# Early token planes, loads at step heads and staggered conversions in a fused attention, gated and normalised layer

## The chip, the cores and the metric

One core of one Trainium2 chip runs the kernel. The metric is device time in microseconds of one execution. TensorE (PE) does the matmuls, VectorE (DVE), ScalarE (ACT) and GpSimd (POOL) the work on elements, and SyncE (SP) issues most DMAs; each engine runs its instructions in order.

## What is computed

```
scores = q @ k.T / 8 + bias(positions)            # 4 batches, 8 heads, 576 tokens, 64 features
x  = softmax(scores) @ v, heads side by side      # 2304 tokens x 512
x2 = ((x @ w1) * (x @ w2)) @ w3 @ w_out           # 512 -> 1024 -> 1024 -> 512
h  = x2 @ w_in;  s = h * softmax(h)               # 1024
out = layernorm(s) * g @ w_out2                   # 2304 x 512
```

All in float32. Weights reach the chip as 64-bit words, and are converted to float32 on it. Products run in float32r as three matmuls, high x high, high x low and low x high: each operand is split into a rounded part (a ScalarE copy) and the rest (a subtraction).

## The kernel before

**Bias** builds the position biases in DRAM. **Attention** runs 16 pairs (two heads of one batch) as one pipeline of slots, ten to a pair: `slot(s)` does scores for one block of keys, the exponent of an earlier one, transposes (`tp`, evicted by L477 on ScalarE and L491 on VectorE) and the product with v (`op`). Its result o is written to `x_d`, for each batch two planes of partial sums (from v's high and low part), two slots after its last matmul, by L453 on SP.

**Gated** takes the 2304 tokens in six chunks (c) of 384 and the 1024 hidden columns in eight blocks (f) of 128. For every chunk, four groups (k) of 128 features are loaded as two planes (`load_x`), added (`sum_x`, L723) and split into high and low (`split_x`, L728 on ScalarE and L730). `stage1(c, f)` is 24 matmuls of 384 columns (L79 to L81) into one of two PSUM tiles `ab`; `gate` copies one half (L768) and multiplies it with the other (L769 on VectorE), which frees the tile, and stores the product to `g_d`. `stage2` reads it back (`gl`) and multiplies by the folded weights `wf` = w3 @ w_out, which `fold(m)` makes in steps 17 to 24.

Weights are converted between the steps: a conversion (`f64`) loads raw words into one of four buffers (`raw`), then does L69 on ScalarE and L70 to L73 on VectorE, a rounding on ScalarE (L637) and a subtraction on VectorE (L640). `convert(n)` does n such pieces, turn by turn for the two oldest conversions, so that these run in lockstep; `feed` starts new ones, whose loads are issued on SP and wait there for a buffer.

From slot 160 on (n = s - 160, `early(n)`) the last pair's slots and the first gated steps share the engines. Chunk 0's planes are loaded at n = 0, added at n = 2 to 5 and split at 3 to 6; chunk 1's go into the tiles of `wf` at n = 8 (MID), all of this arithmetic but the rounding on GpSimd. EARLY puts three products between the slots. `run` then does a step per (c, f), chunks 0 and 1 in turn: gates, stage 1, fold, conversions, stage 2, and at the end of a step a piece of the next chunk's tokens (`next_x`): planes of k = 2, 3 loaded at f = 2 and added at 3, planes of k = 0, 1 loaded at f = 4 and added at 5, splits at 6 and 7. **Solu** does the last layer.

Of the kernel before, what the change touches and what calls it, by code (L numbers as in the profile page):

```python
# [23 lines left out]
TC = 384  # L24
# [178 lines left out]
class Attention:  # L203
# [228 lines left out]
    def values(self, n, u, s):  # L432

        nc, w = self.nc, self.W[n]
        (p, b), (h, c) = self.pairs[n], u
        if c == 0:
            w["op"] = self.ops.tile([128, 2, 512], F, tag="op", name="op")
        for x in range(2):
            for half in range(2):
                js = slice(half * HS, half * HS + HS)  # L440
                if c < 4:
                    lhs, rhs = w["v"][:, h * 4 + c, :], w[("et", h)][x][:, c, js]
                else:

                    lhs, rhs = w["v"][:, 8 + h, :], w["etl"][x][:, js]
                nc.tensor.matmul(w["op"][:, half, :HS], lhs, rhs, start=c == 0 and x == 0, stop=c == 4 and x == 1)  # L446
        if c == 4:
            o, ps = self.ep.tile([128, S], F, tag="o", name="o", bufs=2), w["op"]
            self.OUT.append((halves(o), ps[:, :, :HS]))

            def out():
                for x in range(2):
                    self.ch.load(self.x_d[b][x, p * 128 + h * 64 : p * 128 + h * 64 + 64], o[64 * x : 64 * x + 64])  # L453

            self.at(s + 2, out)
# [64 lines left out]
class Gated:  # L520
# [8 lines left out]
    EARLY = {7: (0, 0), 10: (0, 1), 14: (1, 0)}  # L529
    MID = 8  # L530

    def __init__(self, ch, i, x_d, x2_d, gw_d, g_d):
        self.ch, self.nc, self.i = ch, ch.nc, i
        self.x_d, self.x2_d, self.gw_d, self.g_d = x_d, x2_d, gw_d, g_d
        self.left, self.tail, self.right, self.psl, self.psr = (contextlib.ExitStack() for _ in range(5))
        self.full = []
        self.M, self.freed = {}, 0
        self.AB, self.W3, self.X, self.XS, self.PS, self.G, self.WF, self.XP = ({} for _ in range(8))
        self.W = [None] * 8
        self.place, self.XC = {}, {}  # L540
        self.queue, self.active, self.turn, self.done, self.outs, self.count = [], [], 0, set(), [], 0

    def open_keep(self):
        self.kp = self.ch.pool(self.left, "gq")
        self.wo = self.pp = None
        self.rests, self.stores = [], []
        self.raw_ab = self.kp.tile([128, 4, 1024], U, name="rab", tag="big1")
# [59 lines left out]

    def convert(self, n):

        stuck = []  # L610
        while n > 0:
# [5 lines left out]
            e = go[self.turn % min(2, len(go))]  # L617
# [84 lines left out]
    def spot(self):  # L702
        t = self.xp.tile([128, 2, TC], R, tag="x", name="x", bufs=6)
# [15 lines left out]

    def sum_x(self, c, r, pool, tag, bufs):  # L720
        t = pool.tile([128, TC], F, tag=tag, name="xs", bufs=bufs)
        eng = self.nc.vector if c > 1 else self.nc.gpsimd
# [9 lines left out]
    def next_x(self, c, f):  # L732

        X = self.X
        if f == 2:
            for k in range(2):
                X[(c, k)] = self.spot()
                self.load_x(c, k + 2, X[(c, k)])
        elif f == 3:
            for k in range(2):  # L740
                self.XS[(c, k + 2)] = self.sum_x(c, X[(c, k)], self.xp, "xs", 2)
        elif f == 4:
            for k in range(2):
                self.load_x(c, k, X[(c, k)])
        elif f == 5:
            for k in range(2):
                self.XS[(c, k)] = self.sum_x(c, X[(c, k)], self.gp, "a", 3)
        elif f == 6:
            for k in range(2):
                self.split_x(c, k, self.XS.pop((c, k)), True)  # L750
        elif f == 7:
            for k in (2, 3):
                X[(c, k)] = self.spot()
                self.split_x(c, k, self.XS.pop((c, k)), True)
# [95 lines left out]
    def pair(self, n, r, s):  # L850
# [4 lines left out]
        else:  # L855
            tile = lambda shape, tag, bufs: self.xp.tile(shape, R, name="xc", tag=tag, bufs=bufs)
            t = [tile([128, 2, 2, 128], "x", 6) for _ in range(6)]
# [95 lines left out]
    def early(self, n):  # L953

        if n == 0:
            self.queue += [(self.cv_ab, f, w) for f in range(1, 8) for w in range(2)]
# [3 lines left out]
        if n == 0:  # L960
            for k in range(4):
                self.X[(0, k)] = self.spot()
                self.load_x(0, k, self.X[(0, k)])
# [4 lines left out]
        if n == self.MID:  # L968

            for k in range(4):  # L970
                t = self.wf(4 + k)
                self.X[(1, k)] = [t[:, 0, :TC], t[:, 1, :TC], t]
                self.load_x(1, k, self.X[(1, k)])
        for k in {10: (0, 1), 12: (2, 3)}.get(n, ()):
            self.XS[(1, k)] = self.sum_x(1, self.X[(1, k)], self.xp, "xs", 2)
        for k in {11: (0, 1), 13: (2, 3)}.get(n, ()):
            self.split_x(1, k, self.XS.pop((1, k)))
        if n > 2:
            self.convert(2 if n < 9 else 3)
        if 2 <= n < 6:  # L980
            self.XS[(0, n - 2)] = self.sum_x(0, self.X[(0, n - 2)], self.xp, "xs", 2)
        if 3 <= n < 7:
            self.split_x(0, n - 3, self.XS.pop((0, n - 3)))
# [7 lines left out]
    def run(self):  # L991
# [7 lines left out]
        self.last = True  # L999
# [5 lines left out]
        for s in range(len(self.EARLY), len(steps) + self.NEAR + 1):  # L1005
# [3 lines left out]
            now = order[s] if s < len(steps) else None  # L1009
            self.put_outs()  # L1010
            for key in list(self.PS):
# [17 lines left out]
            self.put_stores()  # L1029
            self.convert(many - 3)  # L1030
# [12 lines left out]
            if now and s > 7 and now[0] + 1 < NC:  # L1043
                self.next_x(max(2, now[0] + 1), s % 8)
# [297 lines left out]
```

## Time and profile before

| | |
|---|---|
| median of 3 runs | 898.34 us (897.34 to 901.94) |
| the profiled execution | 898.74 us, span 897.0 us |
| PE busy | 855.3 us (95%) |
| DVE, ACT, POOL busy | 633.8, 506.5, 317.6 us |
| attention's last slots and the first gated steps | about 300 to 343 us of the span |
| chunks 0 and 1 | to 400 us |

Times are microseconds from the start of the span. A row of the timeline has start, duration, engine, line, operation, tiles and shapes, the number of instructions merged, and in brackets the idle time of that engine before it and what released it. Rows with a start closer to the last than its duration overlap, since engines pipeline.

### The profile page before, as it was taken

How to read it: one execution, taken by the hardware profiler on the slowest of the kernel's cores; microseconds unless marked ns; L12 is line 12 of the kernel's file. 1: busy time of each engine (PE TensorE's matmuls, PEld its weight loads, DVE VectorE, ACT ScalarE, POOL GpSimd, SP SyncE). 2: the span in 40 equal slices, each digit the busy share in tenths (PEclk: the TensorE clock that was granted, in tenths of full speed). 3: DMA queues.
4: the chain of work that ended last, by engine and by line, in shares of the span. 5: the costliest groups of instructions: out<-in, count | busy, mean ns of one | idle time of the engine just before them, and what ended most of it. 6: DMA issues, size and time to landing. Idle time of an engine off the chain costs nothing.

```text
span 897.0 us, 15995 instructions
## 1 busy us (share of the span) xinstructions
PE 855.3 (95%) x5430; PEld 773.3 (86%) x5430; DVE 633.8 (71%) x1509; ACT 506.5 (56%) x1073; POOL 317.6 (35%) x387
## 2 busy tenths in 40 slices
PE   7979999999999779979999999999999999999998
PEld 3548999999999779978888999999998788888886
DVE  8998999999999789887763577462454855555552
ACT  6978899999999744443322335232244544444432
POOL 3038888888897650000000000000344433333300
PEclk9998999999999989999999999999999999999999
DMA  6897897897985565656432577553244011111001
GB/s 224 300 308 192 233 259 200 254 254 205 289 232 151 192 208 177 237 194 202 156 109 92 186 271 277 155 189 118 62 136 129 13 42 42 47 48 48 23 24 48
DMA packets 93490, 146.31 MB, mean 163 GB/s; under 512 B 11744, under 2 KB 58208, under 8 KB 93408
## 3 DMA queue, kind: packets, MB, share of 16 engines
q1 hardware_dynamic: 86496, 135.85, 49.3%
q10 hardware_dynamic: 6912, 9.44, 2.9%
q8 instruction: 43, 0.70, 0.3%
q14 instruction: 39, 0.32, 0.1%
HBM read 81.93 MB, written 41.30 MB: 137 GB/s over the span
## 4 chain that ended last, share of the span: by engine, by line
PE 71%; DVE 8%; DMA 7%; issue 2%; ACT 2%; POOL 2%; SPq 1%; POOLq 0%; ACTq 0%; DVEq 0%
PE op L446 7%; PE ab L80 7%; PE ab L79 7%; PE ab L81 7%; PE sp L363 6%; PE tp L403 6%; PE o L80 4%; PE o L79 4%; PE o L81 4%; PE x L80 3%; PE x L81 3%; PE x L79 3%; DMA k<-kr 2%; PE t L1174 2%; PE hx L79 2%
## 5 line engine op out<-in xcount | busy, mean ns | idle before, releaser
L79 PE MATMUL ab<-x,ab 128*128 128x384 f32 x320 | 108.1, 338 | 4.3 <-DVE a L769 3.1
L80 PE MATMUL ab<-x,ab 128*128 128x384 f32 x320 | 107.5, 336 | 0.1
L81 PE MATMUL ab<-x,ab 128*128 128x384 f32 x320 | 107.5, 336 | 0.0
L491 DVE TENSOR_TENSOR etl<-tp,eth 128x512 fp32r<-128x512 f32 (+1 forms) x160 | 99.4, 629 | 10.6 <-ACT eth L477 8.3
L393 POOL TENSOR_SCALAR e<-e,st 128x576 f32<-128x576 f32 x128 | 95.5, 756 | 29.1 <-DVE st L389 26.2
L381 ACT ACTIVATE e<-e,st 128x576 f32<-128x576 f32 x128 | 100.2, 783 | 6.0 <-DVE st L374 6.0
L374 DVE CUSTOM_DVE_ANT_0 e<-sp,bt 128x576 f32<-128x576 f32 x128 | 95.5, 747 | 3.4 <-DMA bt<-bias_d 1.9
L477 ACT CAST eth<-tp 128x512 fp32r<-128x512 f32 (+1 forms) x160 | 85.2, 543 | 17.8 <-PE tp L403 10.7
L403 PE MATMUL tp<-idt,e 128*128 128x128 f32 x576 | 87.8, 275 | 5.3 <-DVE ell L491 3.1
L363 PE MATMUL sp<-k,q 128*128 128x288 f32 x256 | 73.5, 302 | 8.2 <-DVE st L374 6.1
L918 POOL MEMSET onef<- 128x128 f32 x1 | 0.2, 207 | 216.7 <-DVE cm L72 216.7
L403 PEld LDWEIGHTS tp<-idt,e 128*128 128x128 f32 x576 | 69.7, 141 | 7.8 <-DVE ell L491 3.3
L769 DVE TENSOR_TENSOR a<-ab,a 128x384 f32<-128x384 f32 x48 | 26.6, 554 | 65.5 <-ACT a L768 65.4
L363 PE MATMUL sp<-k,qz 128*128 128x288 f32 x256 | 72.4, 298 | 0.0
L446 PE MATMUL op<-eth,v 128*128 128x288 f32 x256 | 65.5, 337 | 0.4 <-ACT o L479 0.4
L79 PEld LDWEIGHTS ab<-x,ab 128*128 128x128 f32 x320 | 60.1, 188 | 6.3 <-DVE a L769 4.8
L80 PE MATMUL x<-gl,wf 128*128 128x384 f32 x192 | 64.7, 337 | 0.5 <-DVE gl L62 0.2
L81 PE MATMUL x<-gh,wf 128*128 128x384 f32 x192 | 64.5, 336 | 0.0
L79 PE MATMUL x<-gh,wf 128*128 128x384 f32 x192 | 64.5, 336 | 0.0
L80 PEld LDWEIGHTS ab<-x,ab 128*128 128x128 f32 x320 | 60.1, 188 | 0.4 <-DVE x L730 0.4
L81 PEld LDWEIGHTS ab<-x,ab 128*128 128x128 f32 x320 | 60.1, 188 | 0.0
L363 PEld LDWEIGHTS sp<-k,q 128*128 128x128 f32 x256 | 48.8, 191 | 10.3 <-DVE st L374 7.0
(210 smaller groups left out, 2317.8 us busy)
## 6 DMA issues: line engine op xcount, KB each, us to landing
bias_d<-rs SPq DMA_DIRECT2D x36, 295.5 KB, 3.9
qkr<-in_qk SPq DMA_DIRECT2D x16, 640.0 KB, 5.5
k<-kr SPq DMA_DIRECT2D x64, 144.0 KB, 5.5
x_d<-o SPq DMA_DIRECT2D x64, 144.0 KB, 4.4
g_d<-a ACTq DMA_DIRECT2D x48, 192.0 KB, 2.4
gl<-g_d SPq DMA_DIRECT2D x48, 192.0 KB, 2.4
q<-qh SPq DMA_DIRECT2D x64, 128.0 KB, 3.0
raw<-in_wo SPq DMA_DIRECT2D x16, 512.0 KB, 5.2
```

The costliest lines, as they stand in the source:

```text
L79: mm(out, a[0], b[0], start=first, stop=False, skip_group_check=more)
L80: mm(out, a[0], b[1], start=False, stop=False, skip_group_check=more)
L81: mm(out, a[1], b[0], start=False, stop=last, skip_group_check=more)
L363: nc.tensor.matmul(ps[:, half, :HS], w[("q", "qz")[x]][:, h, q * 128 : q * 128 + 128], w["k"][:, h, half * HS : half * HS + HS], start=x = ...
L374: self.nc.vector.tensor_tensor_reduce(out=halves(e), in0=ps[:, :, :HS], in1=halves(self.BT[(self.pairs[n][0], k)]), scale=-0.125, scalar=3e38,
L381: self.nc.scalar.activation(e, e, AF.Exp, bias=st[:, c : c + 1], scale=-1.0, accum_out=st[:, 2 + 2 * c : 3 + 2 * c])
L393: self.nc.gpsimd.tensor_scalar(out=e, in0=e, scalar1=st[:, c : c + 1], scalar2=1.0, op0=ALU.mult, op1=ALU.mult)
L403: tr = lambda c, src: nc.tensor.transpose(ps[: src.shape[1], c * 128 : c * 128 + 128], src, self.idt)
L446: nc.tensor.matmul(w["op"][:, half, :HS], lhs, rhs, start=c == 0 and x == 0, stop=c == 4 and x == 1)
L477: self.nc.scalar.copy(hi, src)
L491: self.nc.vector.tensor_tensor(out=lo, in0=src, in1=hi.bitcast(F), op=ALU.subtract)
L769: nc.vector.tensor_tensor(out=a, in0=ps[:, 1, :TC], in1=a, op=ALU.mult)
```

## The change

- The planes of chunk 0 for k = 0, 1, 2 are loaded at n = -18, -16 and -14 into the buffer `rab` (whose raw words have been used), and added there on GpSimd at n = -8, -6 and -4. Only k = 3 is loaded at n = 0, and added at 3. The splits stand at n = 1 to 4, and the first product at n = 6 instead of 7.
- Chunk 1's planes for k = 0, 1 are loaded at n = 0 into two free token tiles; only k = 2, 3 remain at n = 8. Its sums and subtractions go to VectorE, at n = 7 to 13.
- The stores of attention's last three results are issued from ScalarE's queue.
- In `run`, planes are loaded at the head of the steps f = 1 and f = 4; the splits stand between a step's conversions; the sums remain at the end.
- In `run`, `choose` lets the older of two conversions go until it is more than three pieces ahead (two, later), so that they run half a conversion apart.

```diff
@@ values
+                queue = self.nc.scalar if s + 2 > 10 * len(self.pairs) else self.nc.sync
...
-    EARLY = {7: (0, 0), 10: (0, 1), 14: (1, 0)}
+    EARLY = {6: (0, 0), 10: (0, 1), 14: (1, 0)}
...
+    def choose(self, go):
+        if self.apart and len(go) > 1 and go[0]["raw"] and go[1]["raw"]:
+            apart = 3 if go[0]["step"] < 7 else 2
+            return go[go[0]["step"] - go[1]["step"] > apart]
+        return go[self.turn % min(2, len(go))]
...
+    def first_x(self, k):
+        w = self.raw_ab.rearrange("p a b -> p (a b)").bitcast(F)
+        self.xr = self.xr or [(w[:, a : a + TC], w[:, b : b + TC]) for a, b in ((0, TC), (2 * TC, 3 * TC), (4 * TC, 2560))]
+        for x in range(2):
+            self.ch.load(self.xr[k][x], self.x_d[0][x, k * 128 : k * 128 + 128, :TC])
...
-        eng = self.nc.vector if c > 1 else self.nc.gpsimd
+        eng = self.nc.vector if c else self.nc.gpsimd
...
+    def x_loads(self, c, f):
+        if f == 1:
+            for k in range(2):
+                self.X[(c, k)] = self.spot()
+                self.load_x(c, k + 2, self.X[(c, k)])
         elif f == 4:
             for k in range(2):
-                self.load_x(c, k, X[(c, k)])
+                self.load_x(c, k, self.X[(c, k)])
...
+        for k in range(3):
+            if n == 2 * k - 18:
+                self.first_x(k)
+            elif n == 2 * k - 8:
+                x = self.xr[k]
+                self.nc.gpsimd.tensor_tensor(out=x[0], in0=x[0], in1=x[1], op=ALU.add)
         if n == 0:
+            for k in range(4):
+                self.X[(0, k)] = self.spot()
+            self.load_x(0, 3, self.X[(0, 3)])
...
+            self.two = [self.spot(4 + k) for k in range(2)]
+            for k in range(2):
+                self.load_x(1, k, self.two[k])
...
-        for k in {10: (0, 1), 12: (2, 3)}.get(n, ()):
-            self.XS[(1, k)] = self.sum_x(1, self.X[(1, k)], self.xp, "xs", 2)
-        for k in {11: (0, 1), 13: (2, 3)}.get(n, ()):
-            self.split_x(1, k, self.XS.pop((1, k)))
+        if n in (7, 8):
+            self.XS[(1, n - 7)] = self.sum_x(1, self.two[n - 7], self.xp, "xs", 2)
+        if n in (9, 10):
+            self.split_x(1, n - 9, self.XS.pop((1, n - 9)), True)
+        if n in (11, 12):
+            self.XS[(1, n - 9)] = self.sum_x(1, self.X[(1, n - 9)], self.xp, "xs", 2)
+        if n in (12, 13):
+            self.split_x(1, n - 10, self.XS.pop((1, n - 10)), True)
...
-        if 2 <= n < 6:
-            self.XS[(0, n - 2)] = self.sum_x(0, self.X[(0, n - 2)], self.xp, "xs", 2)
-        if 3 <= n < 7:
-            self.split_x(0, n - 3, self.XS.pop((0, n - 3)))
+        if n == 3:
+            self.XS[(0, 3)] = self.sum_x(0, self.X[(0, 3)], self.xp, "xs", 2)
+        if 1 <= n < 5:
+            self.split_x(0, n - 1, self.xr[n - 1][0] if n < 4 else self.XS.pop((0, 3)))
...
+            x = (max(2, now[0] + 1), s % 8) if now and s > 7 and now[0] + 1 < NC else None
             self.put_outs()
+            if x:
+                self.x_loads(*x)
...
             self.put_stores()
+            if x:
+                self.x_splits(*x)
             self.convert(many - 3)
...
-            if now and s > 7 and now[0] + 1 < NC:
-                self.next_x(max(2, now[0] + 1), s % 8)
+            if x:
+                self.x_sums(*x)
```

VectorE in attention's last slots, from the last but one eviction of transposes (`etl`) on. Before:

```order
L491 TENSOR_TENSOR etl<-tp,eth 128x512
L73 SCALAR_TENSOR_TENSOR cm<-raw,cm 128x512 x2
L491 TENSOR_TENSOR etl<-tp,eth 128x512
L640 TENSOR_TENSOR ab_5070<-cm,ab_5070 128x512 x2
L70 TENSOR_SCALAR cm<-cm 128x512 x2
L71 TENSOR_SCALAR cm<-cm 128x512
L769 TENSOR_TENSOR a<-ab,a 128x384
L71 TENSOR_SCALAR cm<-cm 128x512
L72 SCALAR_TENSOR_TENSOR cm<-raw,cm 128x512 x2
L73 SCALAR_TENSOR_TENSOR cm<-raw,cm 128x512 x2
```

Now, with the sums at L743, the splits' subtractions at L750, the conversion's at L650, the gate at L791:

```order
L492 TENSOR_TENSOR etl<-tp,eth 128x512
L743 TENSOR_TENSOR xs<-x 128x384
L73 SCALAR_TENSOR_TENSOR cm<-raw,cm 128x512 x2
L492 TENSOR_TENSOR etl<-tp,eth 128x512
L743 TENSOR_TENSOR xs<-x 128x384
L750 TENSOR_TENSOR wf_5066<-xs,wf_5066 128x384
L650 TENSOR_TENSOR ab_5076<-cm,ab_5076 128x512 x2
L70 TENSOR_SCALAR cm<-cm 128x512 x2
L71 TENSOR_SCALAR cm<-cm 128x512
L791 TENSOR_TENSOR a<-ab,a 128x384
L750 TENSOR_TENSOR wf_5067<-xs,wf_5067 128x384
L71 TENSOR_SCALAR cm<-cm 128x512
```

The sums and subtractions for chunk 1, which stood on GpSimd, now stand between VectorE's evictions and the weights' last piece.

SP from the raw words of `ab` on, before:

```order
L47 DMA raw<-in_w 128x4x256 x6
L47 DMA raw<-in_wo 128x1024 x6
L47 DMA x<-x_d_60 128x2x384 x2
L47 DMA raw<-in_wo 128x1024 x2
L47 DMA raw<-in_w3t 128x4x256 x2
L47 DMA x<-x_d_60 128x2x384 x2
L47 DMA raw<-in_w3t 128x4x256 x4
```

Now:

```order
L47 DMA raw<-in_w 128x4x256 x8
L47 DMA raw<-in_wo 128x1024 x4
L47 DMA x<-x_d_60 128x2x384 x2
L47 DMA raw<-in_wo 128x1024 x4
L47 DMA x<-x_d_60 128x2x384 x2
L47 DMA raw<-in_w3t 128x4x256 x7
```

Two raw loads fewer stand ahead of each of chunk 2's pairs of planes.

VectorE in the steps before chunk 2, before, over two gates:

```order
L769 TENSOR_TENSOR a<-ab,a 128x384
L73 SCALAR_TENSOR_TENSOR cm<-raw,cm 128x512
L640 TENSOR_TENSOR big_5547<-cm,big_5546 128x512 x2
L70 TENSOR_SCALAR cm<-cm 128x512 x2
L71 TENSOR_SCALAR cm<-cm 128x512 x2
L769 TENSOR_TENSOR a<-ab,a 128x384
```

Now:

```order
L791 TENSOR_TENSOR a<-ab,a 128x384
L72 SCALAR_TENSOR_TENSOR cm<-raw,cm 128x512
L650 TENSOR_TENSOR big_5518<-cm,big_5517 128x512
L73 SCALAR_TENSOR_TENSOR cm<-raw,cm 128x512
L70 TENSOR_SCALAR cm<-cm 128x512
L71 TENSOR_SCALAR cm<-cm 128x512
L72 SCALAR_TENSOR_TENSOR cm<-raw,cm 128x512
L650 TENSOR_TENSOR big_5518<-cm,big_5517 128x512
L73 SCALAR_TENSOR_TENSOR cm<-raw,cm 128x512
L791 TENSOR_TENSOR a<-ab,a 128x384
```

The pairs of equal pieces are taken apart: between one conversion's L73 and its subtraction now stand three pieces of the next.

## Rows read from the trace of the kernel before

**Rows 1.** Timeline of PE, 311 to 344 us.

```profile
311.94 1.11 PE L403 MATMUL tp<-idt,e 128*128 128x128 f32 x4 [3.06 <-DVE ell L491]
...
317.54 0.34 PE L79 MATMUL ab<-x,ab 128*128 128x384 f32 x1
...
323.31 0.33 PE L79 MATMUL ab<-x,ab 128*128 128x384 f32 x1
...
329.81 0.44 PE L79 MATMUL ab<-wf,ab 128*128 128x384 f32 x1 [2.18 <-ACT wf L728]
...
335.70 0.69 PE L80 MATMUL ab<-wf,ab 128*128 128x384 f32 x1 [1.03 <-POOL wf L730]
...
339.26 0.34 PE L79 MATMUL ab<-wf,ab 128*128 128x384 f32 x1
...
343.43 0.34 PE L79 MATMUL ab<-x,ab 128*128 128x384 f32 x1
```

**Rows 2.** Timeline of ACT, the first split of chunk 0.

```profile
310.16 0.51 ACT L728 CAST x<-xs 128x384 fp32r<-128x384 f32 x1 [2.30 <-POOL xs L723]
```

**Rows 3.** Timeline of POOL, 293 to 329 us.

```profile
293.40 0.75 POOL L393 TENSOR_SCALAR eab<-eab,st 128x576 f32<-128x576 f32 x1 [3.47 <-DVE st L389]
...
311.14 1.00 POOL L730 TENSOR_TENSOR x<-xs,x 128x384 fp32r<-128x384 f32 x1
...
328.23 2.05 POOL L723 TENSOR_TENSOR xs<-wf 128x384 f32<-128x384 f32 x2 [10.08 <-DMA wf<-x_d]
```

**Rows 4.** Windows: busy by engine, granted clock, DMA share, GB/s.

```profile
310.00:315.00 5.00, 2.85 (x13) 2.51 (x13) 3.81 (x6) 3.54 (x7) 4.78 (x6) 0.68 0.34 130
335.00:340.00 5.00, 4.30 (x16) 4.30 (x17) 4.50 (x7) 1.84 (x5) 2.06 (x2) 0.59 0.23 73
360.00:380.00 20.00, 20.00 (x117) 20.00 (x116) 17.13 (x35) 9.01 (x17) 0.00 (x0) 1.00 0.72 246
385.00:390.00 5.00, 5.00 (x25) 5.00 (x25) 4.83 (x11) 1.67 (x4) 0.00 (x0) 0.81 0.63 185
```

**Rows 5.** Timeline of DVE, 311 to 343 us.

```profile
311.80 1.77 DVE L70 TENSOR_SCALAR cm<-cm 128x512 f32<-128x512 f32 x2
...
316.38 2.31 DVE L72 SCALAR_TENSOR_TENSOR cm<-raw,cm 128x512 uint32<-128x512 uint32 x2
...
319.22 1.28 DVE L73 SCALAR_TENSOR_TENSOR cm<-raw,cm 128x512 uint32<-128x512 uint32 x2
...
321.02 1.28 DVE L640 TENSOR_TENSOR ab<-cm,ab 128x512 fp32r<-128x512 f32 x2
...
342.91 0.75 DVE L71 TENSOR_SCALAR cm<-cm 128x512 uint32<-128x512 uint32 x2
```

**Rows 6.** Timeline of PE, waits from 382 to 404 us.

```profile
382.86 0.44 PE L79 MATMUL ab<-wf,ab 128*128 128x384 f32 x1 [1.82 <-DVE a L769]
...
395.01 0.44 PE L79 MATMUL ab<-wf,ab 128*128 128x384 f32 x1 [1.99 <-DVE a L769]
...
400.27 0.45 PE L79 MATMUL ab<-x,ab 128*128 128x384 f32 x1 [0.82 <-DVE a L769]
...
403.80 0.44 PE L79 MATMUL ab<-x,ab 128*128 128x384 f32 x1 [1.18 <-ACT x L728]
```

**Rows 7.** Timeline of DVE, sums of planes in chunks 0 and 1.

```profile
381.32 1.02 DVE L723 TENSOR_TENSOR xs<-x 128x384 f32<-128x384 f32 x2
...
393.05 0.56 DVE L723 TENSOR_TENSOR xs<-x 128x384 f32<-128x384 f32 x1 [3.22 <-DMA x<-x_d]
```

**Rows 8.** Timeline of SP (DMA issues; a merged row holds its waits).

```profile
304.86 11.11 SPq L47 DMA_DIRECT2D x_d<-o  x4
...
321.83 6.03 SPq L47 DMA_DIRECT2D wf<-x_d  x8
...
386.67 1.01 SPq L47 DMA_DIRECT2D x<-x_d  x2
```

**Rows 9.** The page's costliest groups: busy, mean ns, idle before.

```profile
L769 DVE TENSOR_TENSOR a<-ab,a 128x384 f32<-128x384 f32 x48 | 26.6, 554 | 65.5 <-ACT a L768 65.4
```

More of the change, by code (lines that the diff above doesn't have):

```diff
@@ L451, in out @@
             def out():
+                queue = self.nc.scalar if s + 2 > 10 * len(self.pairs) else self.nc.sync
                 for x in range(2):
-                    self.ch.load(self.x_d[b][x, p * 128 + h * 64 : p * 128 + h * 64 + 64], o[64 * x : 64 * x + 64])
+                    queue.dma_start(self.x_d[b][x, p * 128 + h * 64 : p * 128 + h * 64 + 64], o[64 * x : 64 * x + 64])
             self.at(s + 2, out)
@@ L536, in __init__ @@
         self.full = []
-        self.M, self.freed = {}, 0
+        self.apart = False
+        self.M, self.freed, self.spots = {}, 0, 0
         self.AB, self.W3, self.X, self.XS, self.PS, self.G, self.WF, self.XP = ({} for _ in range(8))
@@ L546, in open_keep @@
         self.rests, self.stores = [], []
+        self.xr = None
         self.raw_ab = self.kp.tile([128, 4, 1024], U, name="rab", tag="big1")
@@ L616, in convert @@
             self.turn += 1
-            e = go[self.turn % min(2, len(go))]
+            e = self.choose(go)
             r = self.step(e)
@@ L699, in wf, with spot @@
         return self.place[1 if m > 3 else 2].tile([128, 2, 512], dt, name="wf%d" % m, tag="wf%d" % m)
-    def spot(self):
-        t = self.xp.tile([128, 2, TC], R, tag="x", name="x", bufs=6)
+    def spot(self, at=None):
+        if at is None:
+            at = self.spots % 6
+            self.spots += 1
+        t = self.xp.tile([128, 2, TC], R, tag="x%d" % at, name="x")
         return [t[:, 0], t[:, 1], t]
@@ L730, in split_x, with x_sums, x_splits @@
         eng.tensor_tensor(out=t[1], in0=x, in1=t[0].bitcast(F), op=ALU.subtract)
-    def next_x(self, c, f):
-        X = self.X
-        if f == 2:
+    def x_loads(self, c, f):
+        if f == 1:
             for k in range(2):
[L737 to L741, printed above, removed]
+                self.X[(c, k)] = self.spot()
+                self.load_x(c, k + 2, self.X[(c, k)])
         elif f == 4:
             for k in range(2):
-                self.load_x(c, k, X[(c, k)])
+                self.load_x(c, k, self.X[(c, k)])
+    def x_sums(self, c, f):
+        if f == 3:
+            for k in range(2):
+                self.XS[(c, k + 2)] = self.sum_x(c, self.X[(c, k)], self.xp, "xs", 2)
         elif f == 5:
             for k in range(2):
[L747 to L754, printed above, removed]
+                self.XS[(c, k)] = self.sum_x(c, self.X[(c, k)], self.gp, "a", 3)
+    def x_splits(self, c, f):
+        for k in {6: (0, 1), 7: (2, 3)}.get(f, ()):
+            if k > 1:
+                self.X[(c, k)] = self.spot()
+            self.split_x(c, k, self.XS.pop((c, k)), True)
     def stage1(self, c, f):
@@ L856, in pair @@
             tile = lambda shape, tag, bufs: self.xp.tile(shape, R, name="xc", tag=tag, bufs=bufs)
-            t = [tile([128, 2, 2, 128], "x", 6) for _ in range(6)]
+            t = [tile([128, 2, 2, 128], "x%d" % x, 1) for x in range(6)]
             t = [(x[:, 0], x[:, 1]) for x in t] + [tuple(tile([128, 2, 128], "xs", 2) for _ in range(2))]
@@ L960, in early @@
         if n == 0:
-            for k in range(4):
-                self.X[(0, k)] = self.spot()
-                self.load_x(0, k, self.X[(0, k)])
+            self.two = [self.spot(4 + k) for k in range(2)]
+            for k in range(2):
+                self.load_x(1, k, self.two[k])
         while self.rests:
@@ L972, in early @@
                 self.X[(1, k)] = [t[:, 0, :TC], t[:, 1, :TC], t]
+            for k in (2, 3):
                 self.load_x(1, k, self.X[(1, k)])
-        for k in {10: (0, 1), 12: (2, 3)}.get(n, ()):
-            self.XS[(1, k)] = self.sum_x(1, self.X[(1, k)], self.xp, "xs", 2)
-        for k in {11: (0, 1), 13: (2, 3)}.get(n, ()):
-            self.split_x(1, k, self.XS.pop((1, k)))
+        if n in (7, 8):
[6 more added lines that the diff above has]
+            self.split_x(1, n - 10, self.XS.pop((1, n - 10)), True)
         if n > 2:
             self.convert(2 if n < 9 else 3)
-        if 2 <= n < 6:
-            self.XS[(0, n - 2)] = self.sum_x(0, self.X[(0, n - 2)], self.xp, "xs", 2)
-        if 3 <= n < 7:
-            self.split_x(0, n - 3, self.XS.pop((0, n - 3)))
+        if n == 3:
+            self.XS[(0, 3)] = self.sum_x(0, self.X[(0, 3)], self.xp, "xs", 2)
+        if 1 <= n < 5:
+            self.split_x(0, n - 1, self.xr[n - 1][0] if n < 4 else self.XS.pop((0, 3)))
         if n in self.EARLY:
@@ L998, in run @@
         late += [(self.mixed, i) for i in range(7)] + [(self.first_pair,)]
-        self.last = True
+        self.last = self.apart = True
         plan, n, loaded, used = {}, 0, 0, 0
```

## The prediction

> **What bounds the kernel now.** I read the PE timeline at the change of phase first, then the engines that PE waits for there, then the same for the steps around 380 to 405 us, where the next idle rows stand. TensorE is the engine to follow: outside two stretches its rows stand back to back.
>
> The first stretch is the end of attention. Before the transposes at 311.94 PE sits idle 3.06 us, before the first matmul on chunk 1 at 329.81 another 2.18 us, and inside that product once more 1.03 us [rows 1]. The first idle time is named after VectorE, but VectorE waited for ScalarE, and ScalarE for a sum on GpSimd: its copy at 310.16 was held 2.30 us [rows 2]. GpSimd in turn sat until the planes landed; for chunk 1 the row says it outright, 10.08 us idle until the DMA [rows 3]. PE pays a second time: the granted clock was 0.68 over 310 to 315 and 0.59 over 335 to 340 [rows 4], so part of these stretches ran at the lower of the two levels (1.2 and 2.4 GHz). While GpSimd works, VectorE slows: a pair of L70 took 1.77 us, a pair of L72 2.31; without GpSimd a pair of L71 (the same kind as L70) took 0.75 and one of L73 (the same kind as L72) 1.28 [rows 5].
>
> The second stretch is chunk 0 and 1's last steps: PE idles 1.82, 1.99 and 0.82 us at three step heads and 1.18 us inside the first step of chunk 2 [rows 6], with a clock of 0.81 over 385 to 390 [rows 4]. The gate that three of them wait for stands on VectorE behind a sum that waited 3.22 us for its planes [rows 7], whose DMA had been issued only at 386.67 [rows 8].
>
> **Stretch one, the change step by step.** Three sums go to slots -8, -6 and -4 on GpSimd, 1.0 us each by the subtraction of that size [rows 3]. One falls into a gap of 3.47 us [rows 3]; the others push later normalisations by under 1 us, which VectorE's evictions hide. I take 0, and keep 0 to +1. Six small loads pass SP earlier, ahead of the next pair's k; SP was waiting there, so 0. If the cover failed, the scores would start up to 1 us late.
>
> At slots 1 to 4 ScalarE no longer waits 2.30 us, but two copies of about 0.5 us come earlier and two store issues go through its queue; VectorE's chain, which goes through the pair of L70 at 311.80, starts about 1.0 us earlier. GpSimd's five operations of 1.0 us end near 311.7, so one contended pair stays; the pairs of L71 and L72 win 1.02 and 1.03 us; one sum of 0.5 us [rows 7] is new. VectorE finished its pair of L73 at 319.22 + 1.28 = 320.5 [rows 5]; now 320.5 - 1.0 - 2.05 + 0.5 = 318. On PE the product (0,0) stands one slot earlier, at about 314 instead of 317.54, and ends at 318.2, since a product lasts 343.43 - 339.26 = 4.17 us [rows 1]. But the last transposes now come behind it, and VectorE must still evict them (to 319.8), then do a sum, a split (0.5 each) and the pair of L640, 1.28 [rows 5]: 322. So (0,1) starts at 322 instead of 323.31 and ends at 326.2. This is where most of PE's gain so far is lost.
>
> From 322 VectorE's order is four pairs of L70 or L71 (3.0), a pair each of L72 and L73 (2.6), two gates at 0.55 [rows 9], two sums (1.0) and three splits (1.5), about 9 us in all: the last split of chunk 1 is done at 331, and (1,0) ends one k-group (six matmuls, 1.0 us) later at 332, where before it ended at 339.26. It does not wait for planes, I think: only half of the eight wf loads (6.03 us of issue [rows 8]) remain there, behind two raw loads issued when VectorE passes L73 at 318. Before, the first landed 6.4 us after its issue; now the four have landed by 326, just when the sum is due. (1,1) follows at once; then (0,2) needs its first weights, whose copy on ScalarE stands behind two L69 that wait for raw words: 0.5 us. So (0,2) starts at 336.5 instead of 343.43: **-6.9 us**. Bounds: no wait at all gives -11; the planes late as before, -3.
>
> The stores on ScalarE's queue: SP held four of them for 11.11 us [rows 8]. The wait on SP goes, but what stood behind it were raw loads that wait for buffers anyway; 0. The Trainium skill ("DMA: Bandwidth & Descriptors", Issuing engines are not separate DMA queues) says that issuing from several engines saves only sequencer time, as all run on the same 16 DMA engines; by it too this part is worth about 0, which speaks against this part of the change.
>
> **Stretch two.** From (0,2) to the first step of chunk 2 there are 12 products: 400.27 - 343.43 = 56.8 us [rows 1, 6] against 12 x 4.17 = 50.0. The loss is 6.8: 4.6 idle and 2.2 of lower clock. Planes for chunk 2 now go out at step heads, in the order two raw loads earlier, about one to two steps or 4 to 8 us; the wait of 3.22 us is covered, and with it the gates. What is late next is VectorE itself: 17.13 us busy in 20 [rows 4], 3.57 per product of 4.17, and in four of the 12 steps it also has two sums or two splits, 1.02 [rows 7]: 4.6, which is 0.4 too long each time, 1.7 in all. PE has meanwhile used up VectorE's lead by running 6.9 us ahead. Half a conversion apart, ScalarE's rounding of one falls under VectorE's work on the other; the adds and bits are the same, so this removes gaps, not work. I take 2.0 of loss left, chunk 2 starting at 336.5 + 50 + 2 = 388.5: **-4.8**. Bounds: 0 to -8 (the 6.8 and the 1.18). The 1.18 itself I leave: the splits come mid-step, but PE now follows VectorE closely.
>
> **The fold steps and the rest.** Splits now stand in front of the gate in two fold steps, up to 1.0 us on VectorE, partly under stage 2: **+0.2**, bounds -1 to +3. Later PE's rows are back to back and the order of the late pieces around the last stage is the same: 0.
>
> Sum against the profiled execution: 898.74 - 6.9 - 4.8 + 0.2 = 887.2. That execution is 0.4 above the median of the three runs, less than their spread. I say **887**. 0.5%, about 4.5 us, is what a measurement of this kernel can tell from no change.
>
> **Rivals.**
> - VectorE is not the bound: all of stretch two's loss and the best of stretch one go, -11 - 8 + 1 (the fold steps lose a little): about 881. For it: gaps of ScalarE's round trip go with the new distance. Against: 3.57 + 1.02 over 4.17. 0.15.
> - The middle part does not do what it says: SP is in order, the planes' loads stay behind raw loads that wait for buffers, as at 386.67 [rows 8], and the 6.8 us stay: 898.7 - 6.9 = 892. Against: two raw loads fewer stand ahead. 0.20.
> - The gain comes back as VectorE's debt: if a step costs VectorE 4.5 instead of 3.9 in the 12 steps, 12 x 0.35 = 4 us of the early 6.9 is paid back and nothing of the 6.8 won: 895.5. It decides from about 4.2 us a step on. 0.12.
> - GpSimd stops VectorE at a worse place: its five operations now lie over the first two L640, which ran with GpSimd idle before. If these double as L72 did, and the eviction behind them shifts, chain and (0,2) come 1 to 2 us later: 888.5. 0.08. [...]
> - Slower: the reloads of the gate's products (gl) stand on SP among raw loads that are now one long row (seven in the order, before six and two). In the six fold steps with a second stage, a raw load waits for a conversion, and that for a buffer that PE's fold frees. If a gl waits so for a fold, whose 24 matmuls of 512 columns last 4.17 x 512 / 384 = 5.6 us, second stages start late by up to 4 us six times: 898.7 - 11.7 + 24 = 911. It decides when a gl lands later than product and fold, 9.8 us after its step's head. Against: PE has no such wait now. 0.04.
>
> **Numbers.** The forecast has 0.41. Range 880 to 894.5: it takes in the first two rivals, the fourth and the lower edge of the third, and leaves out some 0.17. Faster by over 0.5% (under 893.9): 0.41 + 0.15 + 0.20 + 0.08, less 0.02 for their edges, 0.82; within 0.5%: 0.14; slower: 0.04.
>
> **What would show it.** PE's first product near 314, (0,1) near 322, (1,0) ending near 332, (0,2) near 336.5; no ScalarE wait for GpSimd's sum, no GpSimd row of 10 us before wf; VectorE's pairs of L71 back at 0.75. In stretch two no VectorE sum that waits for a DMA, and VectorE over 90% busy with PE waits for gates of under 1 us. Wrong if (0,2) starts later than 340, if VectorE's sums still wait for planes, or if PE has new waits after 410.

## The result, and the profile after

The changed kernel takes 890.62 us in the median of four runs (888.25 to 891.37), the kernel before 898.58 beside it: a ratio of 0.9905, 95% interval 0.9887 to 0.9922. The forecast was 887, range 880 to 894.5. Direction and range held; the gain is 8.0 us and not the 11.5 that the forecast's terms sum to.

Where the 7.4 us between the two profiled spans (897.0 and 889.6) lie is read from TensorE's timeline, cut at four places that both kernels have: its last wait of 1.1 us for the attention's row sums (called t0 here), the product (0,2), chunk 2's first step (2,0), and chunk 3's second step (3,1). The timeline of PE, before, at t0:

```profile
301.66 0.63 PE L403 MATMUL tp<-idt,e 128*128 128x128 f32 x4 [1.13 <-DVE st L388]
```

and after, from there to chunk 2, against [rows 1, 6]:

```profile
301.01 0.63 PE L403 MATMUL tp<-idt,e 128*128 128x128 f32 x4 [1.12 <-DVE st L388]
...
310.45 0.66 PE L403 MATMUL tp<-idt,e 128*128 128x128 f32 x4 [1.61 <-DVE ell L492]
...
314.36 0.52 PE L79 MATMUL ab<-x,ab 128*128 128x384 f32 x1
...
322.07 0.34 PE L79 MATMUL ab<-x,ab 128*128 128x384 f32 x1
...
323.70 0.45 PE L81 MATMUL ab<-x,ab 128*128 128x384 f32 x1 [1.11 <-DVE ab L650]
...
327.62 0.33 PE L79 MATMUL ab<-wf,ab 128*128 128x384 f32 x1
...
333.04 0.33 PE L79 MATMUL ab<-wf,ab 128*128 128x384 f32 x1
...
337.20 0.34 PE L79 MATMUL ab<-x,ab 128*128 128x384 f32 x1
...
392.76 0.44 PE L79 MATMUL ab<-x,ab 128*128 128x384 f32 x1 [0.39 <-DVE a L791]
```

| us | before | after | difference | forecast |
|---|---|---|---|---|
| start to t0 | 301.66 | 301.01 | -0.65 | 0 |
| stretch one, t0 to (0,2) | 41.77 | 36.19 | -5.58 | -6.9 |
| stretch two, (0,2) to (2,0) | 56.84 | 55.56 | **-1.28** | **-4.8** |
| (2,0) to (3,1) | 99.17 | 99.40 | +0.23 | +0.2 |
| the rest | 397.56 | 397.44 | -0.12 | 0 |

The first row can't be told from chance: t0 lies between 299.6 and 304.0 us in the profiles of this study. Its mean is 301.7 us in the eleven with the early part and 300.5 in the three without, so the 0 to +1 that the prediction kept for the earlier sums is not excluded.

Stretch one went as described, with one addition (TensorE's clock, below). The sums of chunk 0's planes are gone from the gap, ScalarE's first split no longer waits, and GpSimd's five operations end at 311.2. The timeline of POOL, after, answers to [rows 3]; no row of 10 us follows, since chunk 1's planes are now VectorE's:

```profile
305.06 1.01 POOL L750 TENSOR_TENSOR x<-rab,x 128x384 fp32r<-128x384 f32 x1 [0.66 <-ACT x L748]
306.47 1.18 POOL L750 TENSOR_TENSOR x<-rab,x 128x384 fp32r<-128x384 f32 x1 [0.40 <-ACT x L748]
307.62 1.46 POOL L743 TENSOR_TENSOR xs<-x 128x384 f32<-128x384 f32 x1
...
310.22 1.00 POOL L750 TENSOR_TENSOR x<-xs,x 128x384 fp32r<-128x384 f32 x1
```

On DVE, against [rows 5], one contended pair of L70 is left (1.53), and the pairs of L71 and L72 stand at 0.75 and 1.28. The new row is the one at 320.43: VectorE idles 3.26 us for the copy of the transposes that the product (0,0) has pushed back. Chunk 1's sums no longer wait for a transfer. The first two rows are the subtractions beside GpSimd's work:

```profile
306.11 0.68 DVE L650 TENSOR_TENSOR ab<-rab,ab 128x512 fp32r<-128x512 f32 x1
...
307.52 0.68 DVE L650 TENSOR_TENSOR ab<-rab,ab 128x512 fp32r<-128x512 f32 x1
...
310.31 1.53 DVE L70 TENSOR_SCALAR cm<-cm 128x512 f32<-128x512 f32 x2
...
312.36 0.75 DVE L71 TENSOR_SCALAR cm<-cm 128x512 uint32<-128x512 uint32 x2
...
313.63 1.28 DVE L72 SCALAR_TENSOR_TENSOR cm<-raw,cm 128x512 uint32<-128x512 uint32 x2
...
320.43 0.69 DVE L492 TENSOR_TENSOR etl<-tp,eth 128x512 fp32r<-128x512 f32 x1 [3.26 <-ACT eth L478]
...
327.04 0.55 DVE L743 TENSOR_TENSOR xs<-wf 128x384 f32<-128x384 f32 x1
```

Stretch two is where the gain is missing. Its waits for planes went as forecast: SyncE issues the planes of chunk 2 at 363.42 and 376.86, where before the second pair went out at 386.67 [rows 8], and VectorE's only wait left there is the gates' for ScalarE. Counted from (0,2), the second pair goes out after 39.66 us instead of 43.24: 3.6 us earlier, a little under the 4 to 8 of the forecast. PE's waits for gates fell from 4.6 [rows 6] to 3.1 us, the longest 1.2, where the prediction's sign was under 1 us. SyncE's timeline, then VectorE's and PE's waits (us in total, times, longest), after:

```profile
363.42 0.94 SPq L47 DMA_DIRECT2D x<-x_d  x2
...
376.86 0.89 SPq L47 DMA_DIRECT2D x<-x_d  x2
```

```profile
DVE a L791 <- ACT a L790: 2.1, 5, 0.7
```

```profile
PE ab L79 <- DVE a L791: 3.1, 5, 1.2
```

But VectorE's work did not stay what it was. The windows of stretch two, before and after (columns: window, length, then busy time and instructions of PE, PEld, DVE, ACT, POOL, then PE's granted clock, DMA share, GB/s):

```profile
343.43:400.27 56.84, 52.20 (x290) 51.25 (x289) 48.61 (x98) 25.84 (x47) 0.00 (x0) 0.97 0.63 214
```

```profile
337.20:392.76 55.56, 52.44 (x290) 49.35 (x289) 52.41 (x102) 26.81 (x49) 0.00 (x0) 1.00 0.68 221
```

VectorE is busy 52.41 us of 55.56 where it was busy 48.61. It idles 3.15 us, close to the 3.4 that 52 less 48.6 would have left: the waits were priced right, the work was not. In the groups of DVE in that stretch, before and after, the largest difference is one row:

```profile
L640 DVE TENSOR_TENSOR ab<-cm,ab 128x512 fp32r<-128x512 f32 x8 | 5.2, 685 | 0.2
```

```profile
L650 DVE TENSOR_TENSOR ab<-cm,ab 128x512 fp32r<-128x512 f32 x12 | 8.0, 683 | 0.0
```

Up to (2,0) both kernels finish the same 22 conversions. Before, six of them are done by (0,2); after, three, because stretch one is shorter and VectorE there has eight sums and splits of chunk 1 more, 4.4 us in all (four L743 at 0.548 and 0.546, four L750 at 0.549). The difference in counts over the stretch (19 L650 against 16 L640, one L71 and L72 more, one L70 less) is 2.05 + 0.42 + 0.69 - 0.42 = 2.7 of the 3.8 us. The rest does not come from counts; the table below has what each part of the change adds.

### The profile page after: what moved, and what is told of

It is laid out like the page before. It is cut to its first block, busy times and chain, and to the rows that moved or that the text cites. A ratio compares the mean times of both kernels' runs of the same rounds, so it can differ in the third digit from the quotient of the medians.

```text
span 889.6 us, 15987 instructions
## 1 busy us (share of the span) xinstructions
PE 853.7 (96%) x5430; PEld 769.2 (86%) x5430; DVE 638.0 (72%) x1517; ACT 506.0 (57%) x1073; POOL 307.9 (35%) x379
## 4 chain that ended last, share of the span: by engine, by line
PE 78%; DVE 8%; ACT 2%; DMA 2%; issue 2%; SPq 0%; POOL 0%; ACTq 0%; DVEq 0%; POOLq 0%
PE op L446 9%; PE tp L403 8%; PE sp L363 7%; PE ab L79 7%; PE ab L81 7%; PE ab L80 7%; PE o L80 4%; PE o L79 4%; PE o L81 4%; PE x L80 3%; PE x L81 3%; PE x L79 3%; PE hx L79 2%; PE hx L80 2%; PE hx L81 2%
## 5 line engine op out<-in xcount | busy, mean ns | idle before, releaser
L791 DVE TENSOR_TENSOR a<-ab,a 128x384 f32<-128x384 f32 x48 | 26.6, 555 | 63.6 <-ACT a L790 63.3
L1231 ACT ACTIVATE o<-o,st 128x512 f32<-128x512 f32 x18 | 12.4, 688 | 79.5 <-PE o L81 29.4
```

Of the source, the lines that this page charges most:

```text
L791: nc.vector.tensor_tensor(out=a, in0=ps[:, 1, :TC], in1=a, op=ALU.mult)
```

## The experiments

My first theory was another one. In the stagger one conversion's L70, L71 and L72 stand next to each other on VectorE, each reading what the one before wrote, and start 0.45 us apart; in lockstep the two of a pair start 0.335 us apart (a pair of 0.42 us operations takes 0.75 [rows 5]). The timeline of DVE, after:

```profile
360.16 0.42 DVE L70 TENSOR_SCALAR cm<-cm 128x512 f32<-128x512 f32 x1
360.61 0.43 DVE L71 TENSOR_SCALAR cm<-cm 128x512 uint32<-128x512 uint32 x1
361.07 0.69 DVE L72 SCALAR_TENSOR_TENSOR cm<-raw,cm 128x512 uint32<-128x512 uint32 x1
```

So I thought that the stagger itself ate the gain. The rivals were that the stagger pays, and that the gain comes back as work left over for VectorE. The parts of the change were taken apart in both directions. For each kernel the table has the ratio to the kernel before with its interval, and from its profile the two stretches, cut as above. Each stretch is of one execution. The change, its repetition and the change with its stores on SyncE run the same code in stretch two and took 55.56, 54.58 and 54.09 us there; a single difference of less than about 1.5 us is not told from chance.

| kernel | ratio | stretch one | stretch two | DVE busy in it |
|---|---|---|---|---|
| before | 1 | 41.77 | 56.84 | 48.61 |
| stagger alone | 0.9999 [0.9987, 1.0011] | 41.06 | 55.50 | 49.29 |
| heads alone | 0.9983 [0.9967, 0.9999] | 41.86 | 55.28 | 47.64 |
| early part alone | 0.9941 [0.9923, 0.9960] | 34.34 | 59.68 | 51.70 |
| early part, heads | 0.9944 [0.9924, 0.9964] | 34.35 | 57.28 | 50.56 |
| early part, stagger | 0.9956 [0.9940, 0.9971] | 34.34 | 58.01 | 52.14 |
| the change | 0.9905 [0.9887, 0.9922] | 36.19 | 55.56 | 52.41 |
| the change again | 0.9916 [0.9902, 0.9931] | 35.92 | 54.58 | 51.90 |
| the change, stores on SyncE | 0.9898 [0.9878, 0.9918] | 34.31 | 54.09 | 51.50 |
| the change, (0,0) in slot 7 | 0.9872 [0.9859, 0.9885] | 32.66 | 56.07 | 52.65 |
| slot 7, stores on SyncE | 0.9881 [0.9866, 0.9896] | 32.72 | 55.15 | 51.66 |

The three executions of the change's code also show the work left over by its size. Three, four and five conversions were done by (0,2); in stretch two VectorE had 19, 18 and 17 L650 left, was busy 52.41, 51.90 and 51.50 us, and the stretch got shorter each time. The windows of the second and third, against the change's above:

```profile
339.91:394.49 54.58, 52.30 (x289) 49.62 (x288) 51.90 (x101) 26.39 (x48) 0.00 (x0) 1.00 0.70 225
```

```profile
336.28:390.37 54.09, 51.74 (x289) 49.45 (x288) 51.50 (x100) 26.09 (x47) 0.00 (x0) 1.00 0.71 228
```

**The change without the stagger.**

```
-        self.last = self.apart = True
+        self.last = True
```

> Everything of the change but the stagger: both conversions advance in lockstep pairs again. Theory (one conversion's own L70, L71 and L72 stand back to back on VectorE in the stagger and start 0.45 us apart, where pairs start 0.335 us apart, so the stagger costs VectorE about 0.34 us per step): VectorE's L71 pairs take 0.75 us again, the twelve products from (0,2) to chunk 2's first step take 51.5 to 53 us instead of 55.6, and the time is 886.5 to 888.5. Rival (the stagger pays, because it puts other work into ScalarE's round trips): the gaps in front of L72 and L73 come back, the stretch takes 55.6 us or more, and the time is 890.6 to 893.

892.04 us, stretch two 57.28: the rival, and the theory fell as the main cause. VectorE's pairs are cheaper (50.56 us busy, 1.85 less), but it now idles 6.7 us and not 3.15, as its waits in the stretch show:

```profile
DVE a L791 <- ACT a L790: 4.7, 3, 1.8
DVE big L650 <- ACT big L647: 1.8, 1, 1.8
```

The stagger fills ScalarE's round trips and pays about half of that back in VectorE's busy time: -1.7 us of stretch two (-2.7 and -3.2 by the two other executions of the change's code). That this busy time is the neighbours' later starts fits the rows above; it is measured in part only, by the runs with L70 first below.

**The stagger alone, on the kernel before.**

```
+    def choose(self, go):
...
-            e = go[self.turn % min(2, len(go))]
+            e = self.choose(go)
...
-        self.last = True
+        self.last = self.apart = True
```

> The kernel before with nothing but the stagger of the conversions. Theory (dependent operations back to back cost VectorE about 0.34 us per step): the stretch from (0,2) to chunk 2's first step, 56.8 us before, gets 1 to 4 us longer, and the time is 899 to 902. Rival (the stagger hides ScalarE's round trips): the stretch gets 1 to 3 us shorter, and the time is 895 to 897.5.

897.81 us, a ratio of 0.9999: between the two intervals. Stretch two is 1.34 us shorter, as the rival said, yet the time is the same. The stretch from (2,0) to (3,1) took 101.26 us, 2.1 more than before. The next run shows what stands there.

**The change with chunk 2's loads and splits back at the steps' ends.**

```
-        if f == 1:
+        if f == 2:
...
-                self.x_loads(*x)
...
-                self.x_splits(*x)
...
+                self.x_loads(*x)
                 self.x_sums(*x)
+                self.x_splits(*x)
```

> The changed kernel with the loads of chunk 2's planes and GpSimd's splits back at the ends of the steps; the early part and the stagger stay. Theory (the heads took away VectorE's wait for planes, 3.22 us before, and the stretch is otherwise bound by VectorE's work): that wait of a plane sum for a transfer is back with 2 to 4 us, and the time is 892 to 894.5. Rival (the planes' wait had slack beside the stagger, the heads bring nothing): 890 to 891.

894.18 us, as the theory had it. VectorE's wait for planes is back, and behind chunk 2's first matmuls PE waits twice for planes that are split too late: 101.26 us from (2,0) to (3,1) again, against 99.40. VectorE's waits in stretch two, then PE's timeline:

```profile
DVE xs L743 <- DMA x<-x_d: 2.6, 2, 2.1
```

```profile
396.37 0.44 PE L79 MATMUL ab<-x,ab 128*128 128x384 f32 x1 [1.06 <-ACT x L748]
397.94 0.44 PE L80 MATMUL ab<-x,ab 128*128 128x384 f32 x1 [1.13 <-DVE x L750]
```

So the stagger without the heads loses behind (2,0) what it wins in front of it.

**The early part alone**: the edit above and the one without the stagger, in one kernel.

```
-        self.last = self.apart = True
+        self.last = True
...
-                self.x_loads(*x)
...
-                self.x_splits(*x)
```

> The changed kernel with the early part alone: lockstep pairs, and chunk 2's plane loads and splits at the ends of the steps. Theory (the heads and the stagger each leave the other's wait standing: the stagger alone gave no change, and the early part with the stagger 0.9956): what the early part is worth by itself is what the run with both gave, 893 to 895, and VectorE shows both waits again, the plane sum for a transfer with 2 to 4 us and the gates and L650 for ScalarE with 5 us or more. Rival (the early part's 5.6 us reach the end in full, and the stagger without the heads took some of it back): 891 to 893.

893.34 us, inside the theory's interval and near the rival's. The plane sums wait 2.7 us for transfers and the gates and L650 4.9 for ScalarE, the second a little less than the theory said. What decides is stretch two: 59.68 us, 2.84 more than in the kernel before, though nothing in that part of the code was changed. The window:

```profile
336.43:396.11 59.68, 53.48 (x290) 51.11 (x290) 51.70 (x105) 26.46 (x49) 0.00 (x0) 0.97 0.62 213
```

VectorE is busy 3.1 us longer there. The same step from without to with the early part gives +2.9 us busy beside the heads (47.64 to 50.56) and +2.85 beside the stagger (49.29 to 52.14), and makes the stretch 2.0 and 2.5 us longer. That is the work left over, three times over. The heads and the stagger together without the early part were not run, so that what the early part adds beside both is concluded from these three.

**The heads alone, on the kernel before**, with `next_x` cut in three as in the change.

```
             self.put_outs()
+            if x:
+                self.x_loads(*x)
...
             self.put_stores()
+            if x:
+                self.x_splits(*x)
             self.convert(many - 3)
...
-                self.next_x(max(2, now[0] + 1), s % 8)
+                self.x_sums(*x)
```

> The kernel before with nothing but the loads of the planes at the steps' heads and the splits between the conversions. Theory (without the stagger VectorE waits for ScalarE instead): the plane sum's 3.2 us for a transfer are gone, the stretch from (0,2) to chunk 2's first step gets 0 to 2 us shorter than 56.8, and the time is 896 to 898. Rival (the heads by themselves give back the wait they remove): the stretch is 3 us or more shorter and the time is 894 to 895.5.

895.86 us, 0.9983, between the two intervals; stretch two is 1.56 us shorter, as the theory had it. The sum's wait for its planes is gone, and the gates wait for ScalarE 5.3 us instead of 2.7: one wait takes over from the other.

**The product (0,0) in slot 7 again.**

```
-    EARLY = {6: (0, 0), 10: (0, 1), 14: (1, 0)}
+    EARLY = {7: (0, 0), 10: (0, 1), 14: (1, 0)}
```

> The changed kernel with product (0,0) one slot later, in slot 7, where it was before, so that no transposes of the attention stand behind it. Theory (in slot 6 the product pushes head pair 3's transposes back, and VectorE, idle 3.26 us at 320.43 for them, makes AB[1] late): that idle is gone, (0,1) begins at about 320 instead of 322.07, and as the stretch behind is bound by VectorE the gain stays: 888 to 889. Rival (the early part is bound by the attention's other work and its order costs nothing): 890 to 891.

887.11 us: faster than the change, and a little better than the theory's 888 to 889. The transposes come first, and PE's products stand close behind each other:

```profile
311.97 0.66 PE L403 MATMUL tp<-idt,e 128*128 128x128 f32 x4
...
312.98 0.34 PE L79 MATMUL ab<-x,ab 128*128 128x384 f32 x1
...
318.76 0.33 PE L79 MATMUL ab<-x,ab 128*128 128x384 f32 x1
...
322.92 0.33 PE L79 MATMUL ab<-wf,ab 128*128 128x384 f32 x1
```

The product begins 13.39 us behind t0; in slot 6 it was 13.35 in the change and 12.1 in the variants above. But from (0,0) to (0,2) it takes 19.27 us against 22.84 and 22.2. This is the lowest time of the study; its interval overlaps those of two variants of it below (0.9882 and 0.9881).

**The stores of the attention's end on SyncE.**

```
-                queue = self.nc.scalar if s + 2 > 10 * len(self.pairs) else self.nc.sync
+                queue = self.nc.sync
```

> The changed kernel with the last four stores of the attention issued by SyncE again and not by ScalarE's queue. Theory (the first of them waits for the attention's last rows, and the loads behind it on that queue are the weights of the next conversions and chunk 1's planes): SyncE stands 5 us or more at the store, L69 or a plane sum waits for a transfer 2 us or longer, (0,2) begins later than 339, and the time is 892 to 894. Rival (those loads have slack): 890 to 891.

889.41 us, ratio 0.9898 [0.9878, 0.9918]: the rival, 0.6 below its interval. SyncE does stand at the stores (a row of 8.50 us at 305.15), but (0,2) begins at 336.28, and the loads behind them had slack. The stores' queue makes no difference that can be told from noise, as the prediction had it.

**The changed kernel again.** In the profile above stretch one took 36.19 us, in the four variants with the same early part and slot 6 (the last one among them) 34.3.

> The changed kernel again, as it is. Its profiled execution took 36.2 us from the attention's last wait for its row sums to (0,2), while four variants with the same early part took 34.3. Theory (that was the chance of one execution, weights that landed 0.7 us late): this one takes 34 to 35 us, and the stretch behind it 54 to 56. Rival (ScalarE's queue with the stores makes it so): 36 us again. The time is 889 to 891 by both.

890.92 us, ratio 0.9916 [0.9902, 0.9931], and 35.92 us: late weights are not the main cause. They are there in the first profile, on ACT:

```profile
307.54 1.25 ACT L69 ACTIVATE cm<-raw 128x512 f32<-128x512 f32 x2 [0.65 <-DMA raw<-in_w]
```

With this wait the transposes in front of (0,0) begin 11.48 us behind t0; in the repetition, which has no such wait, and in the variants they begin at 11.1. So late weights are 0.4 of the first profile's 1.9 us. The windows of ten microseconds from 8 us behind t0 on, of the change, of its repetition and of the variant with the old places, differ in one column, the clock:

```profile
309.01:319.01 10.00, 7.70 (x40) 7.47 (x41) 7.47 (x13) 4.56 (x9) 2.02 (x3) 0.83 0.44 129
```

```profile
311.99:321.99 10.00, 8.09 (x42) 7.82 (x43) 7.79 (x13) 4.01 (x7) 2.17 (x3) 0.83 0.38 107
```

```profile
308.59:318.59 10.00, 8.07 (x54) 7.79 (x54) 8.23 (x14) 5.04 (x10) 2.16 (x3) 1.00 0.44 128
```

In both profiled executions of the change TensorE ran part of this window at its lower level of 1.2 GHz, in none of the four variants' profiles, though PE had been busy 6.8 of the 8 us ahead of it in all of them; with the same busy time the repetition got through 42 and not 54 matmuls. That is 1.5 to 1.6 us: all that the repetition lost against the variants, and what is left of the first profile's 1.9. It is not the stores' queue: three variants with the stores on ScalarE stayed at 1.00. What sets it off was not found. It may be the execution and not the kernel: each profile is one execution, and the mean clock of the change's ten executions goes from 0.992 to 0.996.

**L70 of the next conversion ahead of this one's L73**, with slot 7, so that L70 and L71 of one conversion are no longer neighbours.

```
-            apart = 3 if go[0]["step"] < 7 else 2
+            apart = 2 if go[0]["step"] in (5, 7) else 3
```

> The changed kernel with product (0,0) in slot 7, and in the stagger the next conversion's L70 goes ahead of this one's L73, so that L70 and L71 of one conversion are no longer neighbours on VectorE. Theory (neighbours that depend on each other start 0.45 us apart, others 0.335 us): L71 starts right behind L73, VectorE's need falls by 0.12 us for each of 16 conversions, the stretch gets 1 to 2 us shorter than 56.1 and the time is 885 to 886.5. Rival (between L73 and L650 only two operations are left to cover ScalarE's copy, not three): VectorE idles in front of L650 and the time is 887 to 889.

888.45 us, ratio 0.9882 [0.9861, 0.9904]: the rival's time, by another way. VectorE did save about what was expected (50.68 us busy instead of 52.65 with one L650 of 0.68 less, so 1.3 us; in the pair below, with equal counts of L650, 0.6), and L650 does not wait for its copy. The gates wait longer instead, 3.5 us against 2.6. The group of the gates in stretch two, with slot 7 alone and with this edit too:

```profile
L791 DVE TENSOR_TENSOR a<-ab,a 128x384 f32<-128x384 f32 x12 | 6.6, 554 | 2.6 <-ACT a L790 2.4
```

```profile
L791 DVE TENSOR_TENSOR a<-ab,a 128x384 f32<-128x384 f32 x12 | 6.7, 555 | 3.5 <-ACT a L790 3.2
```

The profile's stretch was 1.4 us shorter all the same, so the pair was run once more with the stores on SyncE, first without this edit, then with it:

> The changed kernel with product (0,0) in slot 7 and the stores of the attention's end on SyncE. Theory (the stores' queue is worth nothing, the slot 1.7 us by order and about 2 us more where it spares the drop of TensorE's clock in front of (0,0)): the clock stays at 1.00 over the early part, which takes 32.7 us again, and the time is 886.5 to 888. Rival (on SyncE the stores hold up the planes of chunk 1): 888.5 to 890.

> The run before it with L70 of the next conversion ahead of this one's L73 too. Theory (its profile won 1.4 us in the stretch, and the time of the first such run hid that in what executions differ by before the stretch): 1 to 1.5 us less than the run beside it, 885 to 886.5. Rival (what VectorE saves there is taken back behind chunk 2's first step): the same time as the run beside it within 0.5 us.

888.05 us (0.9881 [0.9866, 0.9896]) and 888.12 (0.9890 [0.9871, 0.9909]), with stretch two at 55.15 and 55.05: the order of L70 and L73 makes no difference that can be told. The first lies 0.05 above its theory's interval, with the clock at 1.00 and stretch one at 32.72 as the theory had them; the second is its rival's. Beside the change with its stores on SyncE, slot 7 wins 1.6 us of stretch one; its stretch two is 1.1 longer, which chance alone could make.

**Chunk 2's four plane sums on GpSimd**, with slot 7.

```
-        eng = self.nc.vector if c else self.nc.gpsimd
+        eng = self.nc.vector if c and c != 2 else self.nc.gpsimd
```

> The changed kernel with product (0,0) in slot 7, and the four plane sums of chunk 2 on GpSimd, which is idle in that stretch, in place of VectorE. Theory (the stretch is bound by VectorE's work, 52.65 us of 56.07): VectorE has 2.0 us less to do there, the stretch takes 54 to 55, and the time is 885 to 886.5. Rival (beside a GpSimd operation VectorE's L70 and L71 take three times as long, as in the early part of the kernel before): a pair of L70 or L71 beside each sum of 1.0 us takes 1.5 to 1.8 us and not 0.75, and the time is 886.5 to 888.5.

889.00 us, 0.9900 [0.9886, 0.9914], stretch two 56.78: slower than with slot 7 alone, so the rival, somewhat beyond its 888.5. GpSimd's rows for the second pair of sums, VectorE's beside them, and VectorE's beside the first pair:

```profile
379.77 1.01 POOL L743 TENSOR_TENSOR xs<-x 128x384 f32<-128x384 f32 x1 [10.91 <-DVE cm L72]
381.24 1.56 POOL L743 TENSOR_TENSOR xs<-x 128x384 f32<-128x384 f32 x1 [0.46 <-DMA g_d<-a]
```

```profile
380.26 1.07 DVE L650 TENSOR_TENSOR big<-cm,big 128x512 fp32r<-128x512 f32 x1
...
381.86 1.24 DVE L70 TENSOR_SCALAR cm<-cm 128x512 f32<-128x512 f32 x1
```

```profile
366.16 1.50 DVE L73 SCALAR_TENSOR_TENSOR cm<-raw,cm 128x512 uint32<-128x512 uint32 x1
...
368.03 1.12 DVE L71 TENSOR_SCALAR cm<-cm 128x512 uint32<-128x512 uint32 x1
```

L650 took 1.07 us and not 0.68, L70 1.24 and not 0.42: the two sums of the second pair cost VectorE 0.39 + 0.82 = 1.2 us where doing them itself costs 1.02 [rows 7]. The first pair cost 1.5 (L73 1.50 and not 0.69, L71 1.12 and not 0.43).

## Why the prediction was right and wrong

- **Stretch one: right.** Its marks were forecast at 314, 322, 332 and 336.5 and came at 314.36, 322.07, 333.04 and 337.20. That the product in front of the last transposes is "where most of PE's gain so far is lost" is shown: taking it back gives 1.7 us in stretch one (34.34 to 32.66) where the clock is the same. The size of -6.9 lies between the -5.58 of the change, with the clock at 0.83, and the -7.4 of four variants with it at 1.00. The forecast had no term for the clock behind t0, and that the marks fit so closely is in part luck: counted from t0 they came 0.7 to 1.7 us later than forecast, and t0 itself 0.65 earlier.
- **Stretch two: wrong, and this is the step that failed.** "I take 2.0 of loss left" came to 5.56 (55.56 less 50.0), and to 4.6 and 4.1 in the two other executions of the same code. The working counted VectorE's need per step from the kernel before, 3.57 and 1.02 in four steps; that makes 46.9 us in 12 steps, where the kernel before already had 48.61 and the change has 52.41, more than PE's own 50.0. It said that PE, running ahead, uses up VectorE's lead, and gave that no price. The price is three conversions' ends and a little more, 2.7 to 3.1 us of VectorE work that moves across (0,2), and 2.0 to 2.8 us of stretch two. It also said that the stagger "removes gaps, not work"; in busy time the early part, the heads and the stagger add 3.09, -1.14 and 1.85 us in turn, which is the whole step from 48.61 to 52.41. What heads and stagger bring was near: from the early part alone to the whole change the stretch falls from 59.68 to 55.56, -4.1 (-5.1 and -5.6 by the other two executions), against the -4.8 forecast.
- **Rivals.** "The gain comes back as VectorE's debt", given 0.12, had the right mechanism, at a smaller size: 52.41 us in 12 steps are 4.4 us a step, near its 4.5, but the waits did go, so that 890.6 and not 895.5 came out. That the heads would not move the loads is refuted by SyncE's rows. That VectorE is not the bound is refuted by 52.41 of 55.56. Of the forecast's signs of being wrong none came: (0,2) started before 340, no sum waited for planes, and PE has no new wait after 410.
- **GpSimd beside the first L640** (now L650) did not come. The two rows beside GpSimd's took 0.68 us each, at 306.11 and 307.52, and GpSimd's own (306.47 and 307.62) took 1.18 and 1.46 instead of 1.0 [rows 3]. The Trainium skill ("SBUF — State Buffer", Who interferes with whom) says that the one which issues first keeps the shared ports for its whole instruction and the other stands still; VectorE was first here, and in the run with the sums on GpSimd it was second and L650 took 1.07. The trace agrees with that. The rival asked only whether GpSimd lies over L640, and left out which of the two issues first.
- **Fold steps and the rest: right.** +0.23 and -0.12 against +0.2 and 0. No new wait of the second stage: PE's waits between 405 and 502 are for gates, 2.5 us in all, before 2.3.

## What to carry to other kernels

When a change shortens one stretch, count what the nearly full engine finished in it before: work that no longer fits is done in the next stretch, and both have to be summed as one. Two waits on the same engine in one loop cover for each other: the early part with the heads or with the stagger gave nothing over the early part alone, with both it gave 0.4% (0.25% in the repetition, whose interval touches that of the early part alone). And compare stretches from an event that both kernels have: t0 itself lay 4.4 us apart in these profiles, more than most of the effects. Where a difference of a stretch is under 1.5 us, profile the same code again before explaining it.

## What the runs showed of the hardware

- VectorE operations that read what the one before wrote started 0.45 us apart, independent ones of the same kind 0.335. Taking one such pair apart in every conversion saved VectorE 0.6 to 1.3 us of busy time in stretch two and made no difference in time that could be told; the gates waited 0.9 us longer for ScalarE.
- A fifth of what stretch one can gain (1.5 to 1.6 us of 7.4) hung on a drop of TensorE's clock: 0.83 over 10 us in both profiled executions of the change, 1.00 in one execution each of four variants with the same early part, three of which differ only later in the program. Whether kernel or execution decides it, and by what, stays open.
- An idle GpSimd is no free place for VectorE's work: two sums there cost VectorE 1.2 to 1.5 us of standing still and saved it 1.02.
